# A fused convolution, SoLU and mixture kernel: its third chunk convolved in float32, and the start rearranged

## The chip, the cores and the metric

The kernel runs on one core of one Trainium2 chip. The time is device microseconds of one execution. A core has five instruction streams that run side by side and wait for each other by semaphores: TensorE (PE; its weight loads are shown as PEld), VectorE (DVE), ScalarE (ACT), GpSimd (POOL) and SyncE (SP), which here issues every DMA. Each stream runs its own instructions in order. Lower is better.

## The reference

The input x has 8 sequences of 4160 rows of 192 numbers. The first half is a causal convolution over 7 rows, with one set of 7 softmaxed weights for each of 8 heads of 24 columns; the second half takes every row of its result through w_in, a SoLU, a layer norm and w_out:

```python
w = np.exp(weight - weight.max(-1)); w = w / (w.sum(-1) + 1e-9)
out = np.einsum('hk,bskhg->bshg', w, x_unf)       # the 7 rows up to s
h = x @ w_in                                      # 33280 x 192 @ 192 x 1024
e = np.exp(h - h_max); sm = e / (e.sum + 1e-9)
solu = h * sm
ln = (solu - mu) / np.sqrt(var + 1e-06) * g_ln
return ln @ w_out                                 # 33280 x 1024 @ 1024 x 192
```

x, weight and g_ln are float32. w_in and w_out reach the kernel as 64-bit floats, which it reads as pairs of 32-bit words and turns into float32 itself.

## The kernel before, in words

**Tiles and chunks.** The 33280 rows are 260 tiles of 128 rows, taken one after the other by `step(i)`. The convolution runs ahead of them in chunks of rows: chunk 0 has the first 1024 rows (tiles 0 to 7), chunk 1 the next 1056 (tiles 8 to 15), and each later chunk 2080 (chunk 2: tiles 16 to 31). A chunk is cut into windows of 112 rows, and its windows are loaded in pieces of five (`xr`, 480 KB each; chunk 0 and 1 have two pieces, chunk 2 four).

**What happens to a chunk.** `load` brings the pieces in. `sum_squares` measures each half piece, on ACT by a squared sum (L172) or, where `peaks` is set, on DVE by a maximum (L166). `add_up` sums that over partitions by a matmul with ones (L83), and `scale_steps` makes from it the scale `s` and four constants `cv` on DVE. `product` convolves (L262): an `exact` chunk multiplies the float32 piece by the float32 taps, 4 heads of one piece to a group; any other chunk first has its windows split into float16 upper and lower halves `xs` (L211 on ACT, L217 and L220 on POOL, `halve_steps`) and multiplies those by `taps_hi` and `taps_lo`, three matmuls for each head. Either way a chunk of 19 windows has eight groups. A group is written to the one bank of pool `ps_c` (tag cv, one buffer), from which `upper` (ACT, L285) and `lower` (DVE, L294) put float16 halves into `y16` (one buffer, shared by all chunks). `open` takes the tile `yT` for the chunk and copies the rows left over from the chunk before; `turn` transposes y16 into yT by DMA (L317), in the pieces that `turns` lists, three blocks to a piece. Before, a chunk is opened and transposed only when its last group is done.

**What happens to a tile.** TensorE: ten matmuls of yT with w_in's halves `whi` and `wlo` into `ph` (`emit_h`, L722). DVE: the scaled minimum (`emit_max`, L733). ACT: the exponential (L740). DVE: the product (`emit_mul`, L793). ACT: the float16 upper half (`emit_hi`, L801) and the square (L805). POOL: the lower half (`emit_lo`, L810). SP: a DMA transpose into pT (L812). TensorE, five steps later: 24 matmuls with w_out's halves `ohi` and `olo` (`emit_out`, L824). DVE: the copy out of the bank (L832). Chains of small DVE steps, the rows and the halving of later chunks are slipped into the steps.

**What sets the order.** The order of each engine is the order in which the code emits (the schedule is manual); `chores` spreads a later chunk's groups, transposes, sums and loads over the steps of a chunk by fractions of its number of tiles. SP's DMAs stand in one queue. Before the first step stand the taps (a band matrix spread by matmuls, L439; their float16 halves `split_taps`, L457 and L468), the conversion of w_in (`Words`: mantissas, exponents, join, powers, signs, value) and the first words of w_out; w_out's own conversion, its mean and its halves run in steps 0 to 2.

Of the kernel before, what the change touches and what calls it, by code (L numbers as in the profile page):

```python
# [19 lines left out]
def kernel(  # L20
# [90 lines left out]
    class Chunk:  # L111
        def __init__(self, ch):
# [7 lines left out]
            self.exact = ch < 2  # L120
            self.peaks = ch > 2
            self.part = None

        def load(self, j):
# [4 lines left out]
                [P, PW, D], F32, name=f"xr_{self.ch}_{j}", tag="xr", bufs=9  # L129
# [216 lines left out]
    for j in range(chunks[0].np):  # L346
        chunks[0].load(j)
    for j in range(NH):
# [67 lines left out]
    for j in range(c0.np):  # L416
        for h in c0.halves(j):
            c0.sum_squares(*h)
# [16 lines left out]
    for a in range(0, NQ, per):  # L435
        bank = tp[:, a // per * 512 : a // per * 512 + per * H * TB]
        for q in range(2 * per):
            j = q // 2
            nc.tensor.matmul(  # L439
                bank[:, j * H * TB : (j + 1) * H * TB], spread(a + j),  # L440
                b16[:, q % 2].rearrange("p h c -> p (h c)"),
                start=q == 0, stop=q == 2 * per - 1,
            )
        act.activation(
            of_blocks(taps, a, a + per),
            bank.rearrange("p (q h c) -> p q h c", q=per, h=H), AF.Copy,
            scale=1.0 / TAPS,
        )

    def split_taps():  # L450
        for a in range(0, NQ, 4):
            t = ps_h.tile([P, F], F32, name=f"tph_{a}", tag="ph")
            for e in range(NH):
                bank = t[:, e * 512 : e * 512 + 4 * H * TB]
                for j in range(2):
                    q = a + 2 * e + j
                    nc.tensor.matmul(  # L457
                        bank[:, 2 * j * H * TB : 2 * (j + 1) * H * TB], spread(q),
                        b16.rearrange("p a h c -> p (a h c)"),
                        start=j == 0, stop=j == 1,  # L460
                    )
            for e in range(NH):
                got = t[:, e * 512 : e * 512 + 4 * H * TB].rearrange(
                    "p (q a h c) -> p a q h c", q=2, a=2, h=H
                )
                for j, to in enumerate((taps_hi, taps_lo)):
                    q = a + 2 * e
                    act.copy(of_blocks(to, q, q + 2), got[:, j])  # L468

    split_taps()  # L470
    c0.add_up()
# [77 lines left out]
    def convolve(a, z, banks):  # L549
        return [  # L550
# [21 lines left out]
    for j, c in enumerate(halves):  # L572
        wi.largest(c, floor[:, j : j + 1])
        words(c)
        if j == 0:
            for f in chain0[1:-4]:
                f()
# [614 lines left out]
```

## Time and profile before

| | us |
|---|---|
| time, median of 3 runs | 1278.97 (1278.03 to 1280.67) |
| time of the profiled execution | 1280.23 |
| its span, first to last instruction | 1278.2 |
| TensorE busy | 1193.7 (93%) |
| VectorE / ScalarE / GpSimd busy | 984.9 / 940.7 / 956.5 |
| TensorE's first tile, minimum begins | 30.27 |
| tile 16 (the first of chunk 2), minimum begins | 150.83 |

In rows of the trace the first number is the start in us from the span's start, the second how long it took (us); then engine, line, operation, what is written and read with its shape, and how many were merged. In brackets stands the idle time ahead of it and what ended it. "SPq" rows are the time that SP spent issuing a DMA. Names carry line numbers of the kernel before; in the changed kernel the same code stands up to 12 lines lower or one higher.

### The profile page before, as it was taken

How to read it: one execution, taken by the hardware profiler on the slowest of the kernel's cores; microseconds unless marked ns; L12 is line 12 of the kernel's file. 1: busy time of each engine (PE TensorE's matmuls, PEld its weight loads, DVE VectorE, ACT ScalarE, POOL GpSimd, SP SyncE). 2: the span in 40 equal slices, each digit the busy share in tenths (PEclk: the TensorE clock that was granted, in tenths of full speed). 3: DMA queues.
4: the chain of work that ended last, by engine and by line, in shares of the span. 5: the costliest groups of instructions: out<-in, count | busy, mean ns of one | idle time of the engine just before them, and what ended most of it. 6: DMA issues, size and time to landing. Idle time of an engine off the chain costs nothing. (4 is left out here: it accounts for less than half of the span.)

```text
span 1278.2 us, 25553 instructions
## 1 busy us (share of the span) xinstructions
PE 1193.7 (93%) x9342; PEld 845.0 (66%) x9342; DVE 984.9 (77%) x2129; ACT 940.7 (74%) x1521; POOL 956.5 (75%) x917
## 2 busy tenths in 40 slices
PE   5666899899999999999999999999899999999997
PEld 3434576677777677776776767676676767767676
DVE  7845798588787988888787878789687877777676
ACT  6765777577778777787877777787776868777774
POOL 2244869597887879798896969798696978857675
PEclk8878999899999999999999999999999999999998
DMA  8384798889999898999979899998979998897988
GB/s 230 58 183 97 145 190 162 168 169 181 208 173 207 159 204 182 192 196 174 213 150 206 164 205 183 172 204 151 206 149 203 189 172 160 152 176 142 188 154 163
DMA packets 724747, 223.05 MB, mean 175 GB/s; under 512 B 650942, under 2 KB 724110, under 8 KB 724622
## 3 DMA queue, kind: packets, MB, share of 16 engines
q1 hardware_dynamic: 724622, 221.43, 91.0%
q8 instruction: 73, 1.20, 0.4%
q14 instruction: 52, 0.43, 0.1%
HBM read 33.00 MB, written 25.56 MB: 46 GB/s over the span
## 5 line engine op out<-in xcount | busy, mean ns | idle before, releaser
L810 POOL TENSOR_TENSOR p<-e,p 128x1024 f16<-128x1024 f32 x257 | 547.8, 2134 | 255.2 <-ACT p L801 254.5
L824 PE MATMUL po<-ohi,pT 128*128 128x192 f16 x4160 | 564.1, 248 | 18.1 <-DMA pT<-p 10.4
L824 PEld LDWEIGHTS <-pT 128*128 128x128 f16 x6240 | 527.8, 99 | 73.3 <-DMA pT<-p 21.6
L824 PE MATMUL po<-olo,pT 128*128 128x192 f16 x2080 | 515.3, 248 | 0.0
L733 DVE TENSOR_SCALAR_CACHE_REDUCE ph<-ph,cv 128x1024 f32<-128x1024 f32 x248 | 319.8, 1289 | 166.3 <-PE ph L722 165.4
L722 PE MATMUL ph<-whi,yT 128*128 128x512 f16 x1560 | 428.1, 384 | 19.2 <-DMA yT<-y 15.2
L722 PEld LDWEIGHTS <-yT 128*128 128x128 f16 x2600 | 252.4, 99 | 275.7 <-DMA yT<-y 18.5
L740 ACT ACTIVATE e<-ph,sm 128x1024 f32<-128x1024 f32 x259 | 287.7, 1111 | 153.8 <-DVE ph L733 147.5
L801 ACT CAST p<-e 128x1024 f16<-128x1024 f32 x259 | 269.4, 1040 | 123.6 <-DVE e L793 73.2
L793 DVE SCALAR_TENSOR_TENSOR e<-ph,cv,e 128x1024 f32<-128x1024 f32 x247 | 315.3, 1276 | 0.0
L722 PE MATMUL ph<-wlo,yT 128*128 128x512 f16 x1040 | 313.3, 383 | 0.9 <-DVE wlo L621 0.9
L805 ACT ACTIVATE sq<-e 128x1024 f32<-128x1024 f32 x259 | 273.3, 1055 | 0.0
L294 DVE SCALAR_TENSOR_TENSOR y<-pc,y 112x456 f16<-112x456 f32 (+2 forms) x150 | 77.6, 534 | 73.0 <-ACT y L285 72.7
L220 POOL TENSOR_TENSOR xs<-xr,xs 128x960 f16<-128x960 f32 (+1 forms) x60 | 115.3, 1921 | 2.4
L832 DVE COPY raw<-po 128x192 f32<-128x192 f32 x257 | 90.2, 351 | 4.2 <-PE po L824 4.2
L285 ACT ACTIVATE y<-pc 112x456 f16<-112x456 f32 (+1 forms) x135 | 65.7, 498 | 31.9 <-PE pc L262 10.7
L262 PE MATMUL pc<-xs,taps_hi 128*112 128x456 f16 x240 | 66.5, 357 | 18.3 <-POOL xs L220 8.7
L166 DVE TENSOR_REDUCE xa<-xr 128x1 f32<-128x384 f32 x112 | 68.6, 619 | 0.0
L217 POOL TENSOR_SCALAR xr<-xr,s 128x960 f32<-128x960 f32 (+1 forms) x60 | 61.5, 1025 | 1.7
L896 DVE TENSOR_SCALAR_CACHE_REDUCE o<-raw,t 128x192 f32<-128x192 f32 x133 | 53.0, 403 | 11.2 <-POOL t L887 11.1
L886 POOL TENSOR_TENSOR t<-t,mhalf 128x8 f32<-128x8 f32 (+3 forms) x34 | 54.3, 1597 | 2.7
L262 PEld LDWEIGHTS <-taps_hi 128*112 128x112 f16 x240 | 31.0, 130 | 35.2 <-issue 9.1
(159 smaller groups left out, 650.6 us busy)
## 6 DMA issues: line engine op xcount, KB each, us to landing
out_dram<-o SPq DMA_DIRECT2D x128, 192.0 KB, 2.7
xr<-in_x_dram SPq DMA_DIRECT2D x41, 480.0 KB, 4.6
xr<-in_x_dram SPq DMA_DIRECT2D x22, 384.0 KB, 4.0
pT<-p SPq DMA_TRANSPOSE x259, 4.5
yT<-y SPq DMA_TRANSPOSE x99, 3.8
raw_out<-in_moe_w_out_dram SPq DMA_DIRECT2D x1, 1536.0 KB
raw_in<-in_moe_w_in_dram SPq DMA_DIRECT2D x2, 512.0 KB, 7.7
xr<-in_x_dram SPq DMA_DIRECT2D x8, 84.0 KB, 2.8
```

The costliest lines, as they stand in the source:

```text
L220: (2.1 * size + 0.2, lambda: pool.tensor_tensor(xl, r, h, ALU.subtract)),
L262: nc.tensor.matmul(o, tp[:, h + j, :], r, start=q == 0, stop=q == len(ops) - 1)
L294: dve.scalar_tensor_tensor(self.at(D, h * HD, e, z, a, b), pc[:, :, e:z], self.scale(), self.at(0, h * HD, e, z, a, b), ALU.mult, ALU.subt ...
L722: nc.tensor.matmul(t.ph[:, n * 512 : (n + 1) * 512], lhs, w[:, r, n * 512 : (n + 1) * 512], start=(j == 0), stop=(j == len(ops) - 1),)
L733: dve.tensor_scalar(t.ph, t.ph, t.cv[:, 0:1], None, ALU.mult, ALU.min, accum_out=t.bias)
L740: act.activation(t.e, t.ph, AF.Exp, bias=t.bias, scale=-1.0, accum_out=grp.z[:, g : g + 1])
L793: dve.scalar_tensor_tensor(t.e, t.ph, t.cv[:, 3:4], t.e, ALU.mult, ALU.mult, accum_out=t.grp.s1[:, t.g : t.g + 1],)
L801: act.copy(t.p16[:, :, 0, :], t.halves)
L805: act.activation(junk, t.e, AF.Square, accum_out=t.grp.s2[:, t.g : t.g + 1])
L810: eng.tensor_tensor(t.p16[:, :, 1, :], t.halves, t.p16[:, :, 0, :], ALU.subtract)
L824: nc.tensor.matmul(t.po[:, 0:D], t.pT[:, a, :], w[:, c, :], start=(j == 0), stop=(j == len(ops) - 1),)
L832: dve.tensor_copy(t.grp.raw[:, t.g, :], t.po[:, 0:D])
```

## The change

1. Chunk 2 becomes `exact` (`ch < 3`): float32 pieces, no `xs`. It also gets `peaks`, so its eight half pieces are measured on DVE (L166) and not on ACT (L172). One more `xr` buffer is kept (10).
2. The convolution of chunks 1 and 2 is spread over other steps, and `open` and each `turn` are put right behind the group that ends a piece. Chunk 1 (with `turns` by loaded pieces) is transposed after its second group, at step 4, and after its fourth, at step 6; before, all of it stood at steps 5 and 6 as three DMAs of ten windows. Chunk 2's groups stand at steps 8 to 13 (8, 8, 9, 10, 11, 11, 12, 13), its transposes at steps 10 and 13. Chunk 2's sums stand at steps 3 to 6 (before 2 to 4), chunk 1's all at step 1 (before 1 and 2).
3. In the start, w_in's first half is loaded ahead of chunk 0's second piece; the words of w_in's last third, and w_out's low words, now come ahead of w_in's float16 halves on ACT; w_out's exponents come ahead of the first minimum on DVE and of GpSimd's sum.
4. Tile 2's w_in matmuls are emitted with tile 1's, ahead of w_out's mean; the sum for w_out's scale goes ahead of the mean too.
5. `split_taps` leaves the start: its matmuls stand at the ends of steps 14 and 15, two quarters in each, in the one bank of `ps_c`.

The diff, cut to its core:

```diff
-            self.exact = ch < 2
-            self.peaks = ch > 2
+            self.exact = ch < 3
+            self.peaks = ch > 1
...
         def turns(self):
-            n = -(-self.nw // 10)
-            cuts = [q * self.nw // n for q in range(n + 1)]
+            if self.exact:
+                cuts = self.cuts if self.np < 3 else [*self.cuts[:-1:2], self.nw]
+            else:
+                n = -(-self.nw // 10)
+                cuts = [q * self.nw // n for q in range(n + 1)]
...
-    split_taps()
-    c0.add_up()
+    for h in c0.halves(1):
+        c0.sum_squares(*h)
+
+    def split_taps(q):
+
+        t = ps_c.tile([P, 512], F32, name=f"tph_{q}", tag="cv")
+        for j in range(2):
+            nc.tensor.matmul(
+                t[:, 2 * j * H * TB : 2 * (j + 1) * H * TB], spread(q + j),
+                b16.rearrange("p a h c -> p (a h c)"), start=j == 0, stop=j == 1,
+            )
+        got = t[:, 0 : 4 * H * TB].rearrange("p (q a h c) -> p a q h c", q=2, a=2, h=H)
+        for j, to in enumerate((taps_hi, taps_lo)):
+            act.copy(of_blocks(to, q, q + 2), got[:, j])
...
+    wi.join(halves[1])
+    wo, W = Words(raw_out, "out"), slice(0, NFC * D)
+    for c in halves:
+        valued(c)
     words(Z)
     wi.powers(Z, bias_in)
-    for c in halves:
-        valued(c)
-    for pc, hg in got0:
-        c0.upper(pc, *hg)
-    valued(Z)
+    wo.lows(W, 2.0**-32)
...
     def out_scale():
+        nonlocal mean
+        mean = ps_o.tile([P, 512], F32, name="mean", tag="po")
...
+            if c.exact:
+                groups, turns = c.groups(), c.turns()
+                put(a, a + 0.01, "open", [c])
+                for blk, y, w in turns:
+                    last = max(j for j, (_, _, _, e) in enumerate(groups) if e <= w)
+                    put(a + (m - a) * last / len(groups), 1.0, "turn", [(c, (blk, y, w))])
+                return
...
-            stage(c1, *((0.375, 0.7, 0.85), (0.19, 0.6, 0.8), (0.25, 0.75, 0.95),
+            stage(c1, *((0.375, 0.875, 1.0), (0.0, 0.75, 1.0), (0.25, 0.75, 0.95),
...
-            emit_h(t)
+            if i != 2:
+                emit_h(t)
+            if i == 1:
+                tiles[2].yT = t.yT
+                emit_h(tiles[2])
...
+        if i in (14, 15):
+            for q in range((i - 14) * NQ // 2, (i - 13) * NQ // 2, 2):
+                split_taps(q)
```

Three places in the order of the engines. First ScalarE in the start, between chunk 0's first evacuation and the first exponential (`e_in` is w_in's exponents, `raw_out` w_out's low words, `whi` the upper halves that tile 0's matmuls read); before:

```order
L526 ACTIVATE e_in<-e_in,bias_in 128x512 x3
L285 ACTIVATE y_0_196<-pr_243,s_193 112x5x96
L285 ACTIVATE y_0_196<-pr_244,s_193 112x5x32
L285 ACTIVATE y_0_196<-pr_244,s_193 112x5x64
L624 CAST whi<-f_in 128x512 x2
L628 CAST whi<-f_in 64x512
L629 CAST whi<-f_in 64x512
L632 CAST whi<-f_in 64x512
L633 CAST whi<-f_in 64x512
L499 ACTIVATE raw_out<-raw_out 128x1536
```

and now:

```order
L520 ACTIVATE e_in<-e_in,bias_in 128x512 x3
L493 ACTIVATE raw_out<-raw_out 128x1536
L620 CAST whi<-f_in 128x512 x2
L625 CAST whi<-f_in 64x512
L626 CAST whi<-f_in 64x512
L629 CAST whi<-f_in 64x512
L630 CAST whi<-f_in 64x512
L285 ACTIVATE y_0_176<-pr_224,s_173 112x5x96
```

The low words moved ahead of all six casts, and chunk 0's second evacuation behind them. On DVE the third of these exponents is now made after the values of both halves of w_in, where it stood ahead of them.

Second SyncE's queue where chunk 1 is transposed (yT is chunk 1's, pT the tiles', xr are loads of chunk 3); before:

```order
L812 DMA_TRANSPOSE pT_642<-p_4_614 128x16x128
L317 DMA_TRANSPOSE yT_653<-y_1_441 128x10x112
L145 DMA xr_3_666<-in_x_dram 128x4x192
L812 DMA_TRANSPOSE pT_676<-p_5_673 128x16x128
L317 DMA_TRANSPOSE yT_653<-y_1_441 128x10x112 x2
L812 DMA_TRANSPOSE pT_735<-p_6_707 128x16x128
```

and now:

```order
L811 DMA_TRANSPOSE pT_538<-p_3_510 128x16x128
L317 DMA_TRANSPOSE yT_478<-y_1_416 128x5x112 x3
L145 DMA xr_2_559<-in_x_dram 128x5x192
L811 DMA_TRANSPOSE pT_602<-p_4_574 128x16x128
L145 DMA xr_3_621<-in_x_dram 128x4x192
L811 DMA_TRANSPOSE pT_640<-p_5_637 128x16x128
L317 DMA_TRANSPOSE yT_478<-y_1_416 128x5x112 x3
L811 DMA_TRANSPOSE pT_696<-p_6_668 128x16x128
```

Three transposes of ten windows became six of five; the first three moved from behind tiles 4 and 5 to behind tile 3, the last three still stand behind tile 5's.

Third ScalarE in steps 14 and 15 (e and p are the tiles', tph the quarters of the taps' halves, xs chunk 3's float16 halves); before:

```order
L740 ACTIVATE e_1143,z_743<-ph_1130,sm_1141 128x1024
L801 CAST p_13_1146<-e_1079 128x2x512
L805 ACTIVATE sq_1179,s_8_745<-e_1079 128x1024
L211 ACTIVATE xs_1115<-xr_2_605,s_914 128x960
L740 ACTIVATE e_1199,z_743<-ph_1185,sm_1197 128x1024
```

and now:

```order
L739 ACTIVATE e_1125,z_701<-ph_1112,sm_1123 128x1024
L800 CAST p_13_1128<-e_1062 128x2x512
L804 ACTIVATE sq_1161,s_8_703<-e_1062 128x1024
L465 CAST taps_hi<-tph_1163 128x2x8x14
L465 CAST taps_lo<-tph_1163 128x2x8x14
L465 CAST taps_hi<-tph_1168 128x2x8x14
L465 CAST taps_lo<-tph_1168 128x2x8x14
L211 ACTIVATE xs_1098<-xr_2_559,s_892 128x960
```

Behind step 14's square stand four casts that stood in the start; on TensorE the matmuls into tph_1168 stand ahead of tile 15's, and write the bank that the casts of tph_1163 read. From tile 17 on the rows of every engine are the same before and after.

More of the change, by code (lines that the diff above doesn't have):

```diff
@@ L448 @@
         )
[L450 to L468, printed above, removed]
-    split_taps()
-    c0.add_up()
+    for h in c0.halves(1):
+        c0.sum_squares(*h)
+    def split_taps(q):
[8 more added lines that the diff above has]
+            act.copy(of_blocks(to, q, q + 2), got[:, j])
     class Words:
```

87 lines of the change are left out of this document (44 added, 43 removed).

## The prediction

> **What bounds the kernel now.** I first asked for busy time by stage. Two stages are shown, from tile 9's minimum to tile 16's and from there to the end (columns: window; length; PE, PEld, DVE, ACT, POOL busy; clock; DMA share; GB/s).
>
> ```profile
> 93.03:150.79 57.76, 43.12 (x276) 27.02 (x275) 35.04 (x74) 34.46 (x54) 31.37 (x27) 0.85 0.53 111
> 150.79:1278.00 1127.21, 1095.24 (x8768) 780.49 (x8766) 886.77 (x1910) 845.41 (x1354) 896.67 (x865) 0.99 0.95 179
> ```
>
> From tile 16 on TensorE is busy 1095.2 of 1127.2 us at clock 0.99: that stage is its own work, and the orders are equal there, so I leave it alone. Before it TensorE is busy 43 of 58 us, and no other engine more. What counts is when tile 16 begins. So the time line of VectorE, at the minima of tiles 0, 3, 8, 9, 14 and 16:
>
> ```profile
> 30.27 1.29 DVE L733 TENSOR_SCALAR_CACHE_REDUCE ph<-ph,cv 128x1024 f32<-128x1024 f32 x1 [1.42 <-PE ph L722]
> 53.30 1.28 DVE L733 TENSOR_SCALAR_CACHE_REDUCE ph<-ph,cv 128x1024 f32<-128x1024 f32 x1
> 93.03 1.29 DVE L733 TENSOR_SCALAR_CACHE_REDUCE ph<-ph,cv 128x1024 f32<-128x1024 f32 x1 [11.25 <-PE ph L722]
> 97.02 1.28 DVE L733 TENSOR_SCALAR_CACHE_REDUCE ph<-ph,cv 128x1024 f32<-128x1024 f32 x1
> 136.74 1.27 DVE L733 TENSOR_SCALAR_CACHE_REDUCE ph<-ph,cv 128x1024 f32<-128x1024 f32 x1
> 150.83 1.29 DVE L733 TENSOR_SCALAR_CACHE_REDUCE ph<-ph,cvm 128x1024 f32<-128x1024 f32 x1 [6.34 <-PE ph L722]
> ```
>
> Now each term, as the time between two of these marks.
>
> **Start to tile 0: later by 4.1.** Rows of the start:
>
> ```profile
> 18.07 1.58 DVE L294 SCALAR_TENSOR_TENSOR y<-pq,s,y 112x320 f16<-112x320 f32 x4
> 19.57 0.42 DVE L493 TENSOR_SCALAR m_in<-raw_in 128x512 int32<-128x512 int32 x1
> 20.36 0.72 ACT L526 ACTIVATE e_in<-e_in,bias_in 128x512 int32<-128x512 int32 x1 [0.83 <-DVE e_in L488]
> 21.56 0.69 DVE L536 TENSOR_TENSOR f_in<-f_in,e_in 128x512 f32<-128x512 f32 x1
> 24.82 2.60 DVE L621 TENSOR_TENSOR wlo<-f_in,whi 128x512 f16<-128x512 f32 x4
> 26.84 0.62 ACT L633 CAST whi<-f_in 64x512 f16<-64x512 f32 x1
> 27.49 1.64 ACT L499 ACTIVATE raw_out<-raw_out 128x1536 f32<-128x1536 uint32 x1
> ```
>
> w_in's first half arrives earlier, its last third does not (the same bytes stand ahead of it), so I let the evacuation at 18.07 stand. Then VectorE has one join and four sign or value steps, 5 at about 0.66: 22.9. Only then the two word steps of the last third (0.35 each as issued): 23.6. ScalarE's third exponents take 0.65 (24.2), the low words 1.6 (25.8), two casts 1.25. VectorE follows them with two lower halves (0.65 each, to 27.8) and the last third's sign and value (1.35): 29.1. Four casts of 0.63: 31.65. Before, the last cast ended at 27.46 and the minimum came 2.8 later; so now at 34.4. Bounds: 2.5 (w_in's data early by 1.5) to 5.
>
> **Tile 0 to tile 3: shorter by 4.6.** w_out's steps on VectorE:
>
> ```profile
> 27.89 0.95 DVE L493 TENSOR_SCALAR m_out<-raw_out 128x1536 int32<-128x1536 int32 x1
> 31.48 3.45 DVE L488 TENSOR_SCALAR e_out<-raw_out 128x1536 int32<-128x1536 int32 x1
> 46.05 0.16 DVE L93 TENSOR_SCALAR t_out<-mean 128x1 f32<-128x1 f32 x1 [1.15 <-PE mean L83]
> ```
>
> The exponents' mask took 3.45 beside GpSimd's sum, a step of the same shape 0.95. It now stands ahead of the first minimum, where VectorE waits for TensorE anyway: 3.45 saved. The wait of 1.15 for the scale's sum goes, its matmul now being ahead of the mean. Tile 2's matmuls move to where TensorE is idle; they cost and save nothing on VectorE, which carries this stage. Tile 3 begins at 34.4 + 23.03 - 4.6 = 52.8. Bounds: 3 to 6.
>
> **Tile 3 to tile 8: 23.0 for 39.7.**
>
> ```profile
> 55.91 0.16 DVE L188 TENSOR_REDUCE xm<-pc 128x1 f32<-128x4 f32 x1 [1.27 <-PE pc L83]
> 57.24 0.14 DVE L193 TENSOR_SCALAR cv<-cv 128x1 f32<-128x1 f32 x1
> 59.87 0.35 DVE L832 COPY raw<-po 128x192 f32<-128x192 f32 x1
> 61.78 0.84 DVE L294 SCALAR_TENSOR_TENSOR y<-pc,s,y 112x160 f16<-112x160 f32 x2 [1.56 <-ACT y L285]
> 109.16 1.20 DVE L166 TENSOR_REDUCE xa<-xr 128x1 f32<-128x576 f32 x2
> 80.08 2.13 POOL L810 TENSOR_TENSOR p<-e,p 128x1024 f16<-128x1024 f32 x1 [3.41 <-ACT p L801]
> 85.31 2.87 SPq L317 DMA_TRANSPOSE yT<-y  x2
> 88.51 1.89 SPq L812 DMA_TRANSPOSE pT<-p  x1
> yT<-y SPq DMA_TRANSPOSE x99, 3.8
> 90.24 1.89 PE L722 MATMUL ph<-whi,yT 128*128 128x512 f16 x4 [5.18 <-DMA yT<-y]
> ```
>
> ScalarE loses chunk 2's eight squares here, VectorE gains eight maxima (0.6 for a half of 576, taken as 0.4 for 384). VectorE then sets the step: minimum 1.2 (the marks' 1.28, less what overlaps), lower half 0.8, product 1.2 (the minimum's shape), copy 0.35, maxima 1.0 or 1.4. Step 3 with the chain of scales (1.4) and a memset comes to 6.2, step 4 to 4.7, step 5 to 5.1, step 6 (no copy) to 3.8: tile 7 at 72.6, before 79.0. Tile 8 waits for chunk 1's first transposes. Tile 3's product ends at 62.2, its cast (1.05) at 63.4, GpSimd at 65.6; SyncE issues its transpose (1.8), then three of five windows (1.45 each, the price of ten windows, my upper bound); the last lands 3.8 after 70.3, and tile 8's remaining matmuls end at 75.8. So the 5.18 wait, and 2.65 of the same kind before it, go. Bounds: 20 (shorter issues) to 29 (steps as before).
>
> **Tile 8 to tile 9: 15.7 for 4.0.** Here the change makes a wait. Chunk 2's first evacuation writes the only y16 buffer, so it needs chunk 1's last transposes done, which stand in SyncE's queue behind tile 5's. Tile 5's product ends at 72.0; cast, GpSimd and SyncE as above give 77.1; the third transpose is issued at 80.0 and lands at 83.8. Behind that evacuation on ScalarE stands tile 8's exponential, behind its bank stands TensorE. Then upper 0.6, lower 0.8, product 1.2, tile 7's cast 1.05, the second group's upper 0.7 and lower 0.8, three maxima 1.4, copies 0.3; TensorE meanwhile is cold, and tile 9's ten matmuls at the cold pace end at about 91.3:
>
> ```profile
> ACT y L285 <- DMA yT<-y: 3.5, 5, 1.7
> 93.63 1.06 PE L722 MATMUL ph<-wlo,yT 128*128 128x512 f16 x2
> ```
>
> Before, this wait was never over 1.7. Tile 9 at 91.5, bounds 9.5 long (no wait, only the chain) to 21.
>
> **Tile 9 to tile 14: 27.4 for 39.7.**
>
> ```profile
> 59.13 1.00 PE L262 MATMUL pc<-xr,taps 128*112 128x120 f32 x8
> 59.96 0.59 PE L722 MATMUL ph<-whi,yT 128*128 128x512 f16 x2
> 156.84 0.59 PE L722 MATMUL ph<-whi,yT 128*128 128x512 f16 x2
> 160.97 0.59 PE L722 MATMUL ph<-whi,yT 128*128 128x512 f16 x2
> ```
>
> A tile without convolution takes TensorE 4.13 (160.97 less 156.84), a float32 group 0.83 (59.96 less 59.13): five steps at 4.96, one more group in step 11, and 0.35 a step for the one bank and the chains make 27.4. GpSimd's halves are no longer waited for. Bounds: 25 to 36.
>
> **Tile 14 to tile 16: 19.5 for 14.1.** The taps' halves have one bank: the second quarter's matmuls wait for ScalarE's casts of the first, and tile 15's matmuls stand behind them.
>
> ```profile
> 11.41 0.35 ACT L468 CAST taps_lo<-tph 128x224 f16<-128x224 f32 x1
> 77.87 1.11 ACT L740 ACTIVATE e<-ph,sm 128x1024 f32<-128x1024 f32 x1 [2.35 <-DVE ph L733]
> 78.97 1.03 ACT L801 CAST p<-e 128x1024 f16<-128x1024 f32 x1
> 79.91 1.06 ACT L805 ACTIVATE sq<-e 128x1024 f32<-128x1024 f32 x1
> 138.40 2.07 ACT L211 ACTIVATE xs<-xr,s 128x960 f16<-128x960 f32 x2
> 148.05 1.89 PE L722 MATMUL ph<-whi,yT 128*128 128x512 f16 x4 [4.04 <-DMA yT<-y]
> ```
>
> From tile 14's minimum: ScalarE is free at 2.6 (two halves of chunk 3 took 2.07 ahead), then exponential, cast, square, two casts: 6.6. Tile 15's matmuls begin at 6.9, 4.5 after TensorE ran dry, take 2.2 and, after such a wait, some 1.6 more: the four after 4.04 idle took 1.89, warm 1.03. Step 14: 10.7. Step 15 has the same wait without the 2.07, after the product: 8.8, of it 0.9 for a cold clock. The old stall of 4.04 for chunk 2's transposes goes, since they are now issued by step 10. Bounds: 15 to 22.
>
> The Trainium skill (TensorE: Matmul & The Clock Gate, Part 1) has the clock halve after one idle window of about 3.4 us. The 4.04 row agrees. By that rule the second wait, some 3.4 by my working, may leave the clock alone; the sum would then be 0.9 lower.
>
> **Costed at nothing.** Chunk 2's halving leaves GpSimd (L217, L220) and ScalarE (L211); neither sets a step above, and if GpSimd is late elsewhere it can only gain. Chunk 1's four squares, now all in step 1, lie on ScalarE while VectorE still values w_out, whose upper halves are ScalarE's next work; if VectorE came sooner, they would show. The tenth xr buffer lets two of chunk 3's loads start without waiting for chunk 0; they stand in SyncE's queue between tile 2's and tile 3's transposes, ahead of need, since chunk 3 is measured from step 8. The three transposes more are in the terms of tiles 8 and 9. `out_lower` comes one tile earlier on VectorE, same work. The order from tile 17 on is the same, with the stalls that it has.
>
> **Sum.** +4.1 - 4.6 - 16.7 + 11.7 - 12.3 + 5.4 = -12.4 us at tile 16, kept to the end. The profiled span was 1278.2 in a run of 1280.2, itself 1.3 above the median: 1278.97 - 12.4 = 1266.6, say 1267.
>
> **Rivals.**
> *The new waits are short (chance 0.20).* SyncE's queue runs ahead, so y16 is free when the scale is (tile 8 to 9 in 9.6), and the casts cost 2.5 and not 5.4: another 6.1 and 2.9 off, 1258. For it speaks that chunk 1 is transposed in smaller pieces; against it that tile 5's transpose stands ahead.
> *The y16 wait is longer (0.13).* If steps 3 to 6 keep their old pace, or the DMAs are crowded by chunk 3's loads, chunk 1's last transposes land near 94 instead of 84: 1277. That the first of chunk 1's transposes before were waited for at TensorE for 5.18 speaks for it; that two of them were issued in 2.87 speaks against.
> *The clock stays low, slower (0.12).* Every group waits for one bank. If those gaps keep TensorE cold from tile 9 on, a step takes twice its 4.96: five steps cost 24.8 more, 1292. It decides from half of that, 12.4. For it: clock 0.85 in the old stage, with two cold tiles from 90.24. Against it: gaps in the steps, by my working, are under 1 us. [...]
>
> **How the numbers follow.** My forecast, 1260 to 1274, gets 0.50; 0.05 is left for what I have not named, around no change. A change under 0.2% (2.6 us) can't be told from none. Faster: 0.50 + 0.20 + half of the second rival and a little of the rest, 0.79; same 0.09; slower 0.12. The range takes in the first two rivals: 1256 to 1278.
>
> **What would show it.** Right: tile 0's minimum near 34.4, tile 8's near 76 with no long wait for yT, no GpSimd wait at L262 in chunk 2, a ScalarE wait of some 5 us for a DMA on y at about 84, two TensorE waits of 3 to 5 us on the taps' casts ahead of tiles 15 and 16. Wrong: half-speed matmuls between tiles 10 and 14, or a ScalarE wait on y beyond 10 us.

## The result, and the profile after

| | before | changed |
|---|---|---|
| time, median of 12 runs each | 1280.95 us (1278.03 to 1283.55) | 1274.17 us (1270.28 to 1276.82) |
| ratio, 95% interval | | 0.9948 (0.9935 to 0.9961) |
| the profiled execution, its span | 1280.23, 1278.2 | 1271.92, 1270.2 |

The change makes the kernel 6.8 us faster. The forecast was 12.4 us: the sign held, and 1274.17 lies just above the upper end of the forecast, 1260 to 1274, and inside the wider 1256 to 1278, but the gain is little more than half of the one predicted. Of what was missing, in the mean of two traces of each kernel, the smaller part is in the stages that the prediction summed, the larger in the long stage that it left alone.

The minima of tiles 0, 3, 8, 9, 14 and 16 on VectorE's time line, now:

```profile
33.10 1.29 DVE L732 TENSOR_SCALAR_CACHE_REDUCE ph<-ph,cv 128x1024 f32<-128x1024 f32 x1 [0.99 <-PE ph L721]
52.91 1.28 DVE L732 TENSOR_SCALAR_CACHE_REDUCE ph<-ph,cv 128x1024 f32<-128x1024 f32 x1
77.56 1.29 DVE L732 TENSOR_SCALAR_CACHE_REDUCE ph<-ph,cv 128x1024 f32<-128x1024 f32 x1 [0.43 <-PE ph L721]
95.20 1.27 DVE L732 TENSOR_SCALAR_CACHE_REDUCE ph<-ph,cv 128x1024 f32<-128x1024 f32 x1
122.81 1.29 DVE L732 TENSOR_SCALAR_CACHE_REDUCE ph<-ph,cv 128x1024 f32<-128x1024 f32 x1 [0.98 <-PE ph L721]
141.00 1.29 DVE L732 TENSOR_SCALAR_CACHE_REDUCE ph<-ph,cvm 128x1024 f32<-128x1024 f32 x1 [4.53 <-PE ph L721]
```

Set beside the prediction's terms, and beside a second trace of the same kernel that was taken later (run `e4_afteragain`):

| stage | before | predicted | changed | second trace |
|---|---|---|---|---|
| start to tile 0 | 30.27 | 34.4 | 33.10 | 32.92 |
| tile 0 to 3 | 23.03 | 18.4 | 19.81 | 20.50 |
| tile 3 to 8 | 39.73 | 23.0 | 24.65 | 25.96 |
| tile 8 to 9 | 3.99 | 15.7 | 17.64 | 16.10 |
| tile 9 to 14 | 39.72 | 27.4 | 27.61 | 28.15 |
| tile 14 to 16 | 14.09 | 19.5 | 18.19 | 19.03 |
| tile 16 begins | 150.83 | 138.4 | 141.00 | 142.66 |
| tile 16 to the end of the span | 1127.37 | 1127.4 | 1129.20 | 1131.84 |

A second trace of the kernel before (run `f4_beforeagain`) has tile 16 at 152.94 and 1126.36 from there to the end.

So the prediction was near the time of each stage up to tile 16, with errors of up to 1.9 us (up to 3.0 against the second trace), four of six to the long side. Four stages in the view of busy time by stretch (window; length; PE, PEld, DVE, ACT, POOL busy; clock; DMA share; GB/s):

```profile
52.91:77.56 24.65, 21.82 (x156) 14.71 (x155) 22.63 (x53) 19.47 (x33) 9.40 (x5) 0.96 0.72 136
77.56:95.20 17.64, 6.40 (x39) 4.79 (x38) 7.09 (x22) 6.04 (x12) 4.46 (x3) 0.71 0.79 172
95.20:122.81 27.61, 25.26 (x215) 19.17 (x213) 23.58 (x53) 19.43 (x33) 11.12 (x12) 1.00 0.94 159
141.00:1270.00 1129.00, 1095.30 (x8768) 779.07 (x8765) 887.20 (x1910) 845.36 (x1354) 893.39 (x863) 0.99 0.94 178
```

From tile 9 to 14 TensorE is busy 25.3 of 27.6 us at full clock: the third rival (a clock that stays low) did not come. From tile 8 to 9 it is busy 6.4 of 17.6: that is the new wait. In the last row TensorE has the same work as before, 1095.3 us, and yet the stage is longer.

**The start.** VectorE's evacuation of chunk 0, which the prediction left at 18.07, and ScalarE's last cast ahead of the first minimum:

```profile
16.87 1.59 DVE L294 SCALAR_TENSOR_TENSOR y<-pq,s,y 112x320 f16<-112x320 f32 x4
29.68 0.62 ACT L630 CAST whi<-f_in 64x512 f16<-64x512 f32 x1
```

The evacuation comes 1.20 us earlier. The first of w_in's four loads landed at 6.60 instead of 9.54, the last at 13.92 and before at 13.36: w_in's first half did arrive early, as the prediction said, and VectorE had its first word steps done ahead of the evacuation. That this moves the evacuation, the prediction held only as its lower bound. From there to the end of the last cast it took 13.4 us (predicted 31.65 - 18.07 = 13.6).

**Tile 0 to 3.** w_out's exponents on VectorE, the matmul of the scale's sum on TensorE, and the first step that reads the sum:

```profile
30.73 0.95 DVE L482 TENSOR_SCALAR e_out<-raw_out 128x1536 int32<-128x1536 int32 x1
39.12 0.38 PE L83 MATMUL mean<-osq,ones 128*128 128x1 f32 x2 [0.96 <-DVE osq L666]
45.89 0.16 DVE L93 TENSOR_SCALAR t_out<-mean 128x1 f32<-128x1 f32 x1 [1.19 <-PE mean L685]
```

The exponents' mask takes 0.95 and no longer 3.45, as predicted. But the wait of 1.15 did not go: the sum was done at 39.5, and the step that reads it still waited until 45.89, now for the sixteen matmuls of the mean (L685). The sum and the mean stand in one tile, and its reader waits for the later writer. This is most of the stage's error of 1.4; in the second trace the error is 2.1 and this wait 2.14.

**Tile 3 to 9.** SyncE's DMA issues between tile 5's start and tile 9's, GpSimd's lower half of tile 5 (the third pT row is its transpose), ScalarE's first evacuation of chunk 2, and TensorE's next group:

```profile
66.22 4.57 SPq L811 DMA_TRANSPOSE pT<-p  x1
70.83 3.90 SPq L317 DMA_TRANSPOSE yT<-y  x3
75.46 3.29 SPq L811 DMA_TRANSPOSE pT<-p  x1
79.48 3.18 SPq L811 DMA_TRANSPOSE pT<-p  x1
82.71 3.89 SPq L317 DMA_TRANSPOSE yT<-y  x3
74.95 2.14 POOL L809 TENSOR_TENSOR p<-e,p 128x1024 f16<-128x1024 f32 x1 [4.00 <-ACT p L800]
88.03 0.66 ACT L285 ACTIVATE y<-pc,s 112x480 f16<-112x480 f32 x1 [9.03 <-DMA yT<-y]
89.72 1.91 PE L262 MATMUL pc<-xr,taps 128*112 128x120 f32 x8 [11.24 <-DVE y L294]
```

SyncE issues one DMA behind another here for 20.4 us, with two loads in the gaps. Chunk 1's transposes cost 1.30 each (predicted at most 1.45), but the tiles' transposes cost 4.57, 3.29 and 3.18 where the prediction put 1.8. It had taken 1.89, which stood in the kernel before at 88.51; the row nearer to its use, between chunk 1's own transposes, was this one of before:

```profile
82.24 2.98 SPq L812 DMA_TRANSPOSE pT<-p  x1
```

GpSimd ended tile 5 at 77.09, 1.8 later than in the prediction's working (75.3), and SyncE began its transpose another 2.4 later, at 79.48, since it was still issuing what stood ahead. So SyncE's queue, more than the products of the tiles, set when chunk 1's last transpose was issued; y16 came free at 88.0 instead of 83.8.

**Tile 14 to 16.** TensorE ahead of tiles 15 and 16:

```profile
129.09 0.35 PE L459 MATMUL tph<-b,shift 20*128 20x224 f16 x2 [4.04 <-ACT taps_lo L465]
130.38 1.91 PE L721 MATMUL ph<-whi,yT 128*128 128x512 f16 x4
138.35 0.35 PE L459 MATMUL tph<-b,shift 20*128 20x224 f16 x2 [2.70 <-ACT taps_lo L465]
139.50 1.03 PE L721 MATMUL ph<-whi,yT 128*128 128x512 f16 x4
```

Both predicted waits are there. Four matmuls took 1.91 behind 4.04 us of waiting and 1.03 behind 2.70, so the second wait did not cool the clock and the 0.9 set aside for it was not spent. That is what the Trainium skill (TensorE: Matmul & The Clock Gate, Part 1) has, with its idle window of about 3.4 us; this trace agrees.

### The profile page after: what moved, and what is told of

It reads as the page before. It is cut to its first block, busy times and chain, and to the rows that moved or that the text cites. A ratio compares the mean times of both kernels' runs of the same rounds, so it can differ in the third digit from the quotient of the medians.

```text
span 1270.2 us, 25628 instructions
## 1 busy us (share of the span) xinstructions
PE 1188.0 (94%) x9382; PEld 843.9 (66%) x9382; DVE 988.3 (78%) x2144; ACT 932.6 (73%) x1504; POOL 945.5 (74%) x909
## 5 line engine op out<-in xcount | busy, mean ns | idle before, releaser
L823 PE MATMUL po<-ohi,pT 128*128 128x192 f16 x4160 | 562.6, 247 | 17.8 <-DMA pT<-p 13.7
L294 DVE SCALAR_TENSOR_TENSOR y<-pc,y 112x456 f16<-112x456 f32 (+2 forms) x140 | 72.4, 534 | 58.5 <-ACT y L285 55.1
L220 POOL TENSOR_TENSOR xs<-xr,xs 128x960 f16<-128x960 f32 (+1 forms) x56 | 107.6, 1922 | 2.3
L285 ACT ACTIVATE y<-pc 112x456 f16<-112x456 f32 (+2 forms) x126 | 61.3, 498 | 18.8 <-DMA yT<-y 5.7
L166 DVE TENSOR_REDUCE xa<-xr 128x1 f32<-128x384 f32 x120 | 73.2, 619 | 0.0
L262 PE MATMUL pc<-xs,taps_hi 128*112 128x456 f16 x224 | 61.6, 356 | 8.8 <-DVE xm L188 6.2
L217 POOL TENSOR_SCALAR xr<-xr,s 128x960 f32<-128x960 f32 (+1 forms) x56 | 57.4, 1026 | 1.7
L213 POOL TENSOR_SCALAR xs<-xr,s 128x960 f16<-128x960 f32 (+1 forms) x52 | 53.3, 1025 | 0.0
```

What stands on the lines that cost most here:

```text
L166: dve.tensor_reduce(self.part[:, col : col + 1], self.raw[j][:, a:z, :], AX.XY, ALU.max, apply_absolute_value=True,)
L220: (2.1 * size + 0.2, lambda: pool.tensor_tensor(xl, r, h, ALU.subtract)),
L294: dve.scalar_tensor_tensor(self.at(D, h * HD, e, z, a, b), pc[:, :, e:z], self.scale(), self.at(0, h * HD, e, z, a, b), ALU.mult, ALU.subt ...
L823: nc.tensor.matmul(t.po[:, 0:D], t.pT[:, a, :], w[:, c, :], start=(j == 0), stop=(j == len(ops) - 1),)
```

## The experiments

Each kernel is compared with the kernel before on the same chip; there the median of the kernel before was 1280.6 to 1281.9. "Marks" are the starts of tile 0's and tile 16's minimum, and "40 to 259" is the time from tile 40's minimum to tile 259's, all from the run's own trace.

| run | time, median | ratio (95%) | tile 0 | tile 16 | 40 to 259 |
|---|---|---|---|---|---|
| before | 1280.95 | | 30.27 | 150.83 | 988.55 |
| before, second trace | 1281.3 (one execution) | | 30.29 | 152.94 | 987.67 |
| changed | 1274.17 | 0.9948 (0.9935 to 0.9961) | 33.10 | 141.00 | 991.77 |
| changed, second time | 1274.9 | 0.9945 (0.9927 to 0.9964) | 32.92 | 142.66 | 994.33 |
| y16 of its own | 1266.75 | 0.9893 (0.9875 to 0.9911) | 32.92 | 135.50 | 990.58 |
| taps over four steps | 1263.98 | 0.9867 (0.9852 to 0.9883) | 32.92 | 132.35 | 990.16 |
| both | 1257.97 | 0.9815 (0.9800 to 0.9830) | 33.87 | 126.36 | 991.56 |
| start put back | 1270.38 | 0.9923 (0.9908 to 0.9937) | 31.31 | 141.34 | 991.14 |
| all three | 1255.81 | 0.9798 (0.9776 to 0.9821) | 30.77 | 120.63 | 992.10 |
| before, chunk 1's turns alone | 1276.47 | 0.9955 (0.9940 to 0.9970) | 30.09 | 148.90 | 986.41 |
| changed, chunk 2 in float16 | 1282.98 | 1.0006 (0.9996 to 1.0015) | 37.57 | 154.29 | 988.68 |
| changed, 88 matmuls more | 1269.30 | 0.9906 (0.9886 to 0.9925) | 32.92 | 143.14 | 987.51 |
| before, 40 matmuls more | 1285.21 | 1.0036 (1.0024 to 1.0049) | 30.28 | 150.94 | 991.67 |
| both, 88 matmuls more | 1255.26 | 0.9797 (0.9778 to 0.9816) | 32.91 | 125.47 | 990.71 |

### The wait for y16

Chunk 1's y16 is put in a buffer of its own (in the place of one xs buffer, which chunk 2 in float32 doesn't use), so chunk 2's first evacuation no longer waits for chunk 1's transposes:

```diff
-                self.y16 = yp.tile(
-                    [CW, NB, NWM, P], F16, name=f"y16_{self.ch}", tag="y16", bufs=1
-                )
+                if self.ch == 1:
+                    own = xp.tile([P, 2 * NWM * D], F16, name="y16_1", tag="xs", bufs=2)
+                    self.y16 = own[0:CW, 0 : NB * self.nw * P].rearrange(
+                        "p (b w q) -> p b w q", b=NB, q=P
+                    )
+                else:
+                    self.y16 = yp.tile(...)
```

> The changed kernel with one edit: chunk 1's y16 lies in a buffer of its own (one that chunk 2's float16 halves no longer use), so that chunk 2's first evacuation does not wait for chunk 1's last transposes. Theory (the y16 wait holds tile 9): the ScalarE wait of 9.0 us goes, tile 8's minimum to tile 9's falls from 17.6 to about 9 us, tile 16 begins about 8.5 us earlier (132.5), and the time falls from 1274.2 to about 1266. Rival (the wait only covers others): GpSimd's copy of the left-over rows still waits for the same transposes and the float32 groups still share one bank, so steps 9 to 13 take longer by as much; tile 16 within 2 us of 141, time 1272 to 1276.

Tile 8's and 9's minimum, and between them the evacuation, which now comes ahead of chunk 1's last transposes:

```profile
79.46 1.29 DVE L738 TENSOR_SCALAR_CACHE_REDUCE ph<-ph,cv 128x1024 f32<-128x1024 f32 x1
81.67 0.66 ACT L291 ACTIVATE y<-pc,s 112x480 f16<-112x480 f32 x1 [0.41 <-issue]
84.28 3.89 SPq L323 DMA_TRANSPOSE yT<-y  x3
88.84 1.27 DVE L738 TENSOR_SCALAR_CACHE_REDUCE ph<-ph,cv 128x1024 f32<-128x1024 f32 x1
```

The stage takes 9.38 (changed: 17.64 and 16.10), and the time falls by 7.4. This confirms the cause and the size of the wait, and the 9.6 that the first rival named for the stage without it. Tile 16 begins at 135.50 and not at the 132.5 expected: it is 5.5 and 7.2 earlier than in the two traces of the changed kernel.

### The taps' halves

```diff
-        if i in (14, 15):
-            for q in range((i - 14) * NQ // 2, (i - 13) * NQ // 2, 2):
-                split_taps(q)
+        if i in (14, 15, 16, 17):
+            split_taps(2 * (i - 14))
```

> The changed kernel with one edit: one quarter of the taps' halves at the end of each of steps 14 to 17, in place of two each at the ends of 14 and 15. Theory (the second quarter in the one bank holds TensorE): both TensorE waits on the taps' casts (4.0 and 2.7 us) and the cold matmuls behind them go; tile 14's minimum to tile 16's falls from 18.2 to about 9, the time from 1274.2 to about 1265. Rival (ScalarE is the limit there, with chunk 3's halves and the casts): the stage falls to 14 at most, and the time to 1270.

TensorE's second part of the halves, and the minima of tiles 14 and 16:

```profile
123.28 1.29 DVE L732 TENSOR_SCALAR_CACHE_REDUCE ph<-ph,cv 128x1024 f32<-128x1024 f32 x1 [0.98 <-PE ph L721]
129.69 0.36 PE L459 MATMUL tph<-b,shift 20*128 20x224 f16 x2
132.35 1.29 DVE L732 TENSOR_SCALAR_CACHE_REDUCE ph<-ph,cvm 128x1024 f32<-128x1024 f32 x1 [1.25 <-PE ph L721]
```

With one part to a step no matmul waits for a cast, and the stage takes 9.07 instead of 18.19 to 19.03; the time falls by 10.2. The two quarters in one step with one bank cost these 10 us, and the same matmuls and casts cost nothing measurable when spread.

### Both together

> The changed kernel with both edits, chunk 1's own y16 and one quarter of the taps' halves a step. Theory (two separate waits on the path, each worth what it measured alone, 7.5 to 8 and 10 to 11 us): tile 16's minimum at about 125, time about 1256. Rival (the second one removed uncovers another limit before tile 16, ScalarE's or GpSimd's halves of chunk 3): tile 16 at 129 or later, time 1260 to 1263.

1257.97 is 16.2 us below the changed kernel, against 7.4 and 10.2 alone: the two add up. The stages 8 to 9 and 14 to 16 take 9.38 and 9.07, as in the single runs.

### The start

The last third's words go ahead of the values of w_in's halves again, and w_out's low words behind the casts:

```diff
-    for c in halves:
-        valued(c)
     words(Z)
     wi.powers(Z, bias_in)
-    wo.lows(W, 2.0**-32)
+    for c in halves:
+        valued(c)
...
+    wo.lows(W, 2.0**-32)
     wo.mantissas(W)
```

> The changed kernel with the start's order on ScalarE and VectorE put back in two places: the words of w_in's last third ahead of the halves' values, and w_out's low words behind w_in's upper halves. Theory (that order is what makes tile 0 late): tile 0's minimum begins at 30 in place of 33.1, and as VectorE carries the stage up to tile 3, tile 3 begins 3 us earlier too (50), and the time falls by 3 us to 1271. Rival (w_out's conversion is the end of that stage): tile 0 begins 3 us earlier, but w_out's integer part and GpSimd's sum come later, and tile 3 begins at 52 to 53 as now; the time stays within 1 us.

Tile 0 begins 1.6 to 1.8 earlier, tile 3 at 51.97 (changed: 52.91 and 53.42). The step that reads the scale's sum waited 2.14 for the mean:

```profile
44.96 0.16 DVE L93 TENSOR_SCALAR t_out<-mean 128x1 f32<-128x1 f32 x1 [2.14 <-PE mean L685]
```

The changed kernel waited as long there in its second trace, and 1.19 in its first, so this wait varies between executions; it does not show that the earlier start makes it longer. Tile 3's mark came out as the rival had it, the time as the theory had it: the median fell by 3.8 to 4.5, more than the 0.9 to 1.5 that the mark shows, and the rest is not explained by the trace, in which tile 16 stands at 141.34.

> The changed kernel with chunk 1's y16 in a buffer of its own, the taps' halves a quarter to a step in steps 14 to 17, and the start's words and w_out's low words put back. Theory, the three add: the first two together came to 1257.97, the third alone took 3.8 us off the time but only 1 to 1.5 off tile 3's mark; by the mark 1256.5, by the time 1254. Rival: behind the earlier start the scale's sum waits longer for w_out's mean, and nothing is left of it: 1257 to 1258.

With the other two edits it came to 1255.81. The ratio, 0.9798 (0.9776 to 0.9821), overlaps that of the two edits alone, 0.9815 (0.9800 to 0.9830). In this one trace tile 0 begins at 30.77 and tile 16 at 120.63, 5.7 earlier than with the two, and the wait for the mean is 0.98, so the rival's longer wait is not there; but this execution, of 1252.78, was the fastest of four, and the median doesn't show as much. How much the order in the start costs is therefore open between 0 and 4 us.

### The parts of the change that were meant for chunks 1 and 2

Chunk 1's transposes alone, put by piece behind their groups in the kernel before:

```diff
+            if self.ch == 1:
+                cuts = self.cuts
...
+            if c.ch == 1:
+                groups, turns = c.groups(), c.turns()
+                put(a, a + 0.01, "open", [c])
+                for blk, y, w in turns:
+                    last = max(j for j, (_, _, _, e) in enumerate(groups) if e <= w)
+                    put(a + (m - a) * last / len(groups), 1.0, "turn", [(c, (blk, y, w))])
+                return
...
-            stage(c1, *((0.375, 0.7, 0.85), ...
+            stage(c1, *((0.375, 0.875, 1.0), ...
```

> The kernel before with one part of the change: chunk 1's transposes in pieces of five windows, each right behind the group that ends it, with its groups spread over steps 3 to 6. Theory (early transposes alone give the gain, chunk 2 in float32 none): tile 8's minimum at 81 to 84 in place of 93.0, tile 16 at 139 to 142, time 1270 to 1273, as the whole change. Rival (chunk 2's float16 halves, made by ScalarE and GpSimd, then hold steps 9 to 12 instead): tile 8 early, tile 16 at 147 to 151, time 1277 to 1281.

Tile 8 begins at 85.89 instead of 93.0, but tile 16 only at 148.90, as the rival expected. The time is 0.9955 (0.9940 to 0.9970) of before, which can't be told from the 0.9948 (0.9935 to 0.9961) of the whole change: with its two waits, the rest of the change added nothing to the time that these runs can show. What was late next is chunk 2's splitting into halves; TensorE's first groups of chunk 2, the second of them behind GpSimd's half:

```profile
94.61 0.54 PE L262 MATMUL pc<-xs,taps_hi 128*112 128x456 f16 x1 [6.59 <-ACT xs L211]
101.78 0.54 PE L262 MATMUL pc<-xs,taps_hi 128*112 128x456 f16 x1 [6.63 <-POOL xs L220]
```

The other way round, the changed kernel with chunk 2 in float16 again (its measuring on ScalarE and its steps as before; the taps' halves must then be made in the start, here a quarter after another in the one bank):

```diff
-            self.exact = ch < 3
-            self.peaks = ch > 1
+            self.exact = ch < 2
+            self.peaks = ch > 2
...
+    for q in range(0, NQ, 2):
+        split_taps(q)
...
-        if i in (14, 15):
-            for q in range((i - 14) * NQ // 2, (i - 13) * NQ // 2, 2):
-                split_taps(q)
```

> The changed kernel with chunk 2 put back to float16 halves: exact and peaks as before, its sums and stages at the steps of before, the taps' halves made in the start. The other parts of the change stay. Theory (float32 is worth its place): without the eight maxima on VectorE and with eight squares on ScalarE steps 3 to 5 take 7 to 9 us each again, and steps 9 to 12 wait for the halves; tile 16 at 145 to 150, time 1276 to 1281. Rival (float32 brings nothing by itself, since it also brings the y16 wait and the taps' waits): tile 16 at 136 to 142, time 1267 to 1273, no slower than the whole change.

It is no faster than the kernel before, and tile 16 begins later than the 145 to 150 expected. Tile 0 begins 4.5 later than in the changed kernel, because of the quarters in one bank: TensorE waits for their casts three times, the first time 2.48 us, and the matmul that chunk 0's scale waits for stands behind them.

```profile
12.46 0.52 PE L459 MATMUL tph<-b,shift 20*128 20x224 f16 x2 [2.48 <-ACT taps_lo L465]
```

From tile 9 to 14 it takes 46.86 us where float32 takes 27.6 and 28.2. Less those 4.5, tile 16 would begin at 149.8, against 141.0 and 142.7 with float32. So float32 for chunk 2 carries 7 to 9 us of the gain at tile 16, and the earlier transposes alone, by the run above, 2 to 4.

### Where the long stage lost time

From tile 17 on the rows of every engine are the same before and after, and TensorE's busy time there is the same. Still, the table shows two groups: the four kernels with chunk 2 in float16 and no matmuls added take 986.4 to 988.7 us from tile 40 to 259, the six with chunk 2 in float32 then known 990.2 to 994.3 (means 987.8 and 991.6). The second traces of both kernels were taken to see whether this repeats:

> The changed kernel itself once more, for a second trace. Theory (the 1.8 us by which the stage from tile 16's minimum to the end is longer than before, 1129.2 for 1127.4, is chance from one execution to the next): the marks up to tile 16 repeat within 0.5 us (141.0), and that stage differs by 1 to 3 us from 1129.2, either way. Rival (the change makes that stage longer): 1129.2 within 0.5 us, in this and in the other kernels that keep the change.

> The kernel before once more, for a second trace. Theory (the stage from tile 16's minimum to the end varies by chance between executions): it differs from 1127.4 by 1 to 4 us. Rival (that stage is fixed for this kernel, and longer in the changed one): 1127.4 within 0.5.

The two groups stay apart, though single traces of one kernel differ more than was expected: tile 16 by 1.7 and 2.1 us (0.5 was expected of the changed kernel), and the stage from there to the end by 2.6 and 1.0. Of the groups of eight tiles from tile 56 on, every second one agrees to 0.2 us in all traces; the groups between them, with the chunks' turns, differ. Waits that are longer, in the changed kernel from tile 40 to 259 (sum, number, longest):

```profile
PE pc L262 <- DVE xm L188: 6.2, 5, 3.0
ACT y L285 <- DMA yT<-y: 5.7, 5, 2.6
```

Before, the same two were 4.1 (longest 1.5) and 3.5 (longest 1.7). The second is a wait for chunk transposes. If the order is the same, something else must meet them at other places. The profile's list of DMA queues has one for instructions, and the rows on engines tell how many TensorE has; before, then after:

```profile
PE 1193.7 (93%) x9342; PEld 845.0 (66%) x9342; DVE 984.9 (77%) x2129; ACT 940.7 (74%) x1521; POOL 956.5 (75%) x917
q8 instruction: 73, 1.20, 0.4%
```

```profile
PE 1188.0 (94%) x9382; PEld 843.9 (66%) x9382; DVE 988.3 (78%) x2144; ACT 932.6 (73%) x1504; POOL 945.5 (74%) x909
q8 instruction: 73, 1.20, 0.4%
```

73 packets for 9342 matmuls and 9342 weight loads are 256 instructions to a packet, and 1.20 MB are 64 bytes to an instruction. The float32 chunk has 40 matmuls more, all ahead of tile 17, so every later packet is fetched 80 instructions earlier in the work. Two kernels move the packets and change no other work, by tiny matmuls in the start, which write a corner of a bank that nobody reads then:

```diff
     tp = ps_h.tile([P, F], F32, name="tps", tag="ph")
+    def idle(n):
+        for _ in range(n):
+            nc.tensor.matmul(
+                tps[0:16, 0:16], shift[:, 0:16], shift[:, 0:16], start=True, stop=True
+            )
+
+    tps = tp
+    idle(40)
...
         ps_c.tile([P, 512], F32, name="pr_1", tag="cv"),
     ]))
+    idle(48)
```

The changed kernel gets both lines, the kernel before only the first.

> The changed kernel with 88 tiny matmuls more on TensorE in the start (40 ahead of the taps' matmuls, where TensorE waits for its first operand, 48 behind chunk 0's last group, in the 7.5 us ahead of tile 0's first matmul); they write a corner of the taps' bank that is not read at that time, nothing else changes. Theory, instruction fetch: TensorE's instructions come by a DMA queue of their own, 73 packets and 1.20 MB for 9342 matmuls and as many weight loads, so a packet holds about 256 instructions; the changed kernel has 40 matmuls more before tile 17 than the kernel before, which moves every later packet by 80 instructions, to other places in the tiles, where it meets other transposes. 88 more make it 256, one whole packet, and the packets stand again where they stood in the kernel before. Then the time from tile 40 to tile 259, 991.8 and 994.3 in the changed kernel's two traces, returns to about 988 (987.7 to 988.7 in the kernels with chunk 2 in float16), and the total falls by 3 to 4 us (ratio about 0.992), give or take the start. Rival, the lengthening hangs on chunk 2's float32 in another way (buffers, timing): it stays at 990 to 994 and the ratio at 0.9945.

> The kernel before with 40 tiny matmuls more on TensorE in the start, ahead of the taps' matmuls, where it waits for its first operand. Theory, instruction fetch: the packets of TensorE's instructions then stand where they stand in the changed kernel, so the time from tile 40 to tile 259 grows from 988 to 990 to 994, and the total by 3 to 4 us (ratio about 1.003), though tile 16 begins as before or up to 1 us later. Rival: 988 stays, ratio 1.000.

The changed kernel with 88 matmuls: its queue, its waits from tile 40 to 259, and the minima of tiles 40 and 259:

```profile
q8 instruction: 74, 1.21, 0.4%
```

```profile
ACT y L285 <- DMA yT<-y: 4.0, 4, 1.4
PE pc L262 <- DVE xm L188: 3.2, 3, 1.4
```

```profile
261.24 1.29 DVE L741 TENSOR_SCALAR_CACHE_REDUCE ph<-ph,cv 128x1024 f32<-128x1024 f32 x1 [1.04 <-PE ph L730]
1248.75 1.29 DVE L741 TENSOR_SCALAR_CACHE_REDUCE ph<-ph,cv 128x1024 f32<-128x1024 f32 x1
```

The kernel before with 40 matmuls more, its time lines of TensorE (the added ones) and VectorE (the same two minima):

```profile
4.66 1.15 PE L437 MATMUL tps<-shift 20*16 20x16 f16 x40 [4.66 <-POOL shift L384]
...
271.86 1.29 DVE L741 TENSOR_SCALAR_CACHE_REDUCE ph<-ph,cv 128x1024 f32<-128x1024 f32 x1 [1.04 <-PE ph L730]
1263.53 1.29 DVE L741 TENSOR_SCALAR_CACHE_REDUCE ph<-ph,cv 128x1024 f32<-128x1024 f32 x1
```

Adding work makes the changed kernel faster, by 4.9 us, and its stage 987.51; adding less than half as much makes the kernel before slower, by 4.6 us, and its stage 991.67. Tile 16 begins within 0.5 us of a trace of the same kernel without the added matmuls (143.14 and 142.66; 150.94 and 150.83). So the lengthening of the long stage follows the number of TensorE's instructions ahead of it, and not float32 as such.

The traces keep the start of every packet, and they bear this out. Counted in tiles, the first packets behind tile 40 start at 41.2 to 41.3, 44.9 to 45.2 and 48.5 to 48.7 in the six traces with as many TensorE instructions ahead as before, or 256 more (before, chunk 1's turns alone, chunk 2 in float16, the two with 88 matmuls), and at 40.3, 43.2 to 43.6 and 47.4 to 47.6 in the eight others, which have 80 more. One step shows what that does. In the eight, a packet starts 2.6 to 3.3 us behind tile 65's minimum, while a tile's transpose is under way. This transpose lands 1.9 to 2.1 us behind the packet's start, 6.3 to 6.7 us after its issue; ScalarE's cast of tile 65 waits for it, and step 66 takes 5.96 to 6.64 us. In the six, no packet starts there, the transpose lands 4.5 to 4.8 us after its issue, and the step takes 4.71 or 4.72. The cast in the kernel before, the changed kernel, this with 88 matmuls, and the kernel before with 40:

```profile
381.52 1.05 ACT L801 CAST p<-e 128x1024 f16<-128x1024 f32 x1
372.89 1.05 ACT L800 CAST p<-e 128x1024 f16<-128x1024 f32 x1 [2.34 <-DMA pT<-p]
374.41 1.04 ACT L809 CAST p<-e 128x1024 f16<-128x1024 f32 x1 [0.62 <-DMA pT<-p]
386.51 1.05 ACT L809 CAST p<-e 128x1024 f16<-128x1024 f32 x1 [2.15 <-DMA pT<-p]
```

Step 212 goes the same way: it takes 8.44 to 8.76 us in the six traces where a packet starts 2.6 to 2.9 us behind its minimum, 6.99 where one starts 3.45 behind it, and 5.96 to 6.75 in the seven others. What isn't shown is how a packet holds a transpose up, and not every turn goes by the packets: tiles 176 to 184 take 39.1 to 39.8 us in the five traces with chunk 2 in float16 and 37.6 to 38.5 in the nine with float32, whatever matmuls are added. So float32 matters to the long stage at one turn, where it makes it shorter.

The same 88 matmuls in the kernel with both edits:

> The first two of these edits (1257.97 together) with the 88 tiny matmuls in the start. Theory, instruction fetch: its 991.6 us from tile 40 to tile 259 return to about 988, the time to about 1254.5. Rival: 991 stays, 1258.

1255.26 against 1257.97 is in the direction expected, but its stage in the one trace, 990.71, is only 0.9 shorter and stays where the rival had it. Its packets stand where they did in the kernel before, step 66 takes 4.72, but tiles 160 to 168 took 41.1 where the other traces have 38.6 to 40.4, and that is not explained. The ratio, 0.9797 (0.9778 to 0.9816), overlaps that without them. It is, with 1255.81 of the three edits, the fastest version here, 19 us faster than the changed kernel.

## Why the prediction was right or wrong

The prediction's sums come out as it wrote them. Its first window, 93.03 to 150.79, begins at tile 8's minimum and not at tile 9's, as its text has it; no term uses that.

- **Start to tile 0 (+4.1, measured +2.8).** The chain was right; the step that failed is "I let the evacuation at 18.07 stand". It came 1.2 earlier, inside the bounds given.
- **Tile 0 to 3 (-4.6, measured -3.2 and -2.5).** The mask's 3.45 was right: it now stands at 30.73, ahead of the first minimum. Wrong is "the wait of 1.15 for the scale's sum goes": a reader of a tile waited for the tile's last writer, so the matmul that went ahead brought nothing.
- **Tile 3 to 8 (-16.7, measured -15.1 and -13.8).** No long wait for yT is left at tile 8, as said. Steps 5 and 6 took 5.87 and 4.29 (7.53 and 4.29 in the second trace) where 5.1 and 3.8 stood.
- **Tile 8 to 9 (+11.7, measured +13.7 and +12.1).** The wait, its place and who stands behind it were right, the experiment shows it; it was 9.03 where some 5 was named. The mis-sized term is SyncE's issue of a tile's transpose, 1.8 taken, 3.2 to 4.6 measured in this crowded stretch; tile 5's lower half, 1.8 late, adds to it. Against the second rival: y16 came free at 88, between the 84 of the forecast and the 94 of that rival.
- **Tile 9 to 14 (-12.3, measured -12.1 and -11.6).** Right in the sum, and no half-speed matmuls. The single steps took 4.55 to 6.82 where the working has 5.3 and, for step 11, 6.1, so part of the close fit is luck.
- **Tile 14 to 16 (+5.4, measured +4.1 and +4.9).** Right in mechanism, shown by spreading the halves. The second wait was 2.70, under the 3.4 of the working, and cost no cold clock.
- **"Kept to the end" (0, measured +1.8 and +4.5).** This is the step that failed most. In the mean of two traces each, tile 16 to the end took 1130.5 instead of 1126.9. The order of the instructions was the same, which the prediction took for the same time; but the instructions ahead of it were 80 more on TensorE, and with them moved the places at which its instructions are fetched. With the packets put back where they were, the kernel takes 1269.3, 11.3 us less than the 1280.58 of before on that chip. That this is close to the 12.4 of the sum is partly luck: in its one trace tile 16 begins at 143.14, 7.7 and 9.8 earlier than in the two traces of before, and the stage from there to the end is 1.3 shorter than their mean.

Of the 5.6 us between forecast and result, then, about 3.7 are the long stage. The rest is in the sum at tile 16: in the mean of two traces each, tile 16 begins 10.1 earlier (141.83 for 151.89), for 12.4. The two parts are 6.0 and not 5.6, since a trace is one execution; single executions of the changed kernel lie 6.5 us apart, so that split is no sharper than 1 or 2 us. The profiled execution of the changed kernel was 2.3 under its median.

## What to carry to other kernels

Price a DMA issue by the rows of the stretch where it will stand, beside the same neighbours, not by the cheapest row of its kind; and where several DMAs follow one another on one queue, add them up before asking when the producer is done. A matmul put ahead of others that write the same tile did not free the tile's reader. And a stage whose instructions and busy times are the same isn't thereby as long: in a kernel whose DMA queues are full, compare runs of a stage, and if it has moved by a few microseconds, try a few idle matmuls in a place where TensorE waits.

## What the runs showed of the hardware that was not expected

The place at which TensorE's instructions are fetched was worth 4 to 5 us of 1280 in two kernels here: 40 matmuls of 0.03 us each, in a place where TensorE waits, made one slower by 0.36% (0.24 to 0.49), and 88 made another faster by 4.9 us. In a third, 88 took 2.7 us off, which is not clear of the noise. A tile's transpose that was under way when a packet of instructions started landed 1.9 to 2.1 us behind that start, 6.3 to 6.7 us after its issue instead of 4.5 to 4.8 (at tile 65, eight traces and six). It is not alone: in the 14 traces from tile 40 to 259, 682 packets start while a transpose issued at least 1 us before is under way. Behind 253 of them the next such transpose lands after 1.75 to 2.25 us, and behind 31 after 0.75 to 1.75; counted from evenly spaced moments and not from packets, it would be 85 and 203.

The Trainium skill (Runtime: NRT & Kernel Launch, Instruction fetch mechanics) has instructions fetched over a DMA queue of the engine's own in blocks of 16 KiB, 256 instructions, at a cost that is mostly hidden. The packets agree: 18,684 instructions in 73. That it is hidden agrees with the 0.4% of the DMA engines' time that the profile shows, but these runs show a cost to the transposes under way.

One tile's transpose (pT) took SyncE from 3.2 to 4.6 us to issue in the crowded stretch and 1.9 in the row of before that the prediction used, while chunk 1's three transposes took 3.9 together both times.
